# Seven-product groups of a fused attention + mixer block: 96-row operand tails, a plan table inside each group, ten tiles instead of eleven summed in DRAM

## The chip, the cores and the metric

The kernel runs on one core of a Trainium2 chip. The metric is the time of one execution in device microseconds (us); lower is better. A core has a matrix engine (TensorE, PE in the profile, with its weight loads shown as PEld), three engines for elementwise work (VectorE = DVE, ScalarE = ACT, GpSimd = POOL) and SyncE (SP), which in this kernel only issues DMA transfers. Every engine works through its own instructions in program order, and each instruction waits for the semaphores of what it depends on.

## The reference, cut to what matters

x is (1, 2048, 576), F = 4608, 32 heads of 18 columns.

```python
xn = layernorm(x)
# A: sliding, dilated attention: each token looks back 8 places, 2 apart
q, k, v = heads(layernorm-input xn @ wqkv)      # 32 heads, Dh = 18
o  = softmax(q . k[s - 0, s - 2, ..., s - 14] * Dh**-0.5) @ v
A  = o @ wo
# B: mixer MLP
h  = gelu(layernorm(xn) @ w1); hs = spatial_shift(h) @ w2     # shifts +1 -1 +2 -2
x1 = xn + hs
B  = x1 + gelu(layernorm(x1) @ w3) @ w4          # w3: 576 x 4608, w4: 4608 x 576
out = x + A + B
```

## The kernel before, in words

All matrix products are made from two fp32r parts: an operand is held as a high part (a cast) and a low part (the operand minus its high part), and high·high + high·low + low·high is summed in PSUM. So each operand costs a cast, which ACT makes, and a subtraction, which DVE makes, before PE may use it.

The time falls into stages: wqkv, w1 and w2 with the layer norms (to about 315 us); then 48 *units* (`for u, (c, b) in enumerate(units)`), which take the first half of F in twelve chunks `c` of 256 hidden columns by four blocks `b` of 512 tokens; then twelve *groups* (`for q in range(NQ)`), which take the second half of F; eight more products behind the groups (the tail); and the last phase, the attention output times wo (L212, sixteen token tiles).

**A unit** makes two `up` products (14 matmuls of 128x512 each, L795), whose gelu ACT takes out of PSUM twice, as the high part (L778) and in full (L779); DVE makes the low part (L789). It then makes four `down` products (12 matmuls of 128x288, L808) with the hidden columns of the unit before. The `down` results are summed per token tile, in one of two ways: for the tiles of `YD` (11 of 16) ACT copies PSUM to a staging buffer (L812) and POOL issues a DMA that accumulates it into DRAM (L813); for the other tiles DVE adds PSUM to a tile that stays in SBUF (L816). PSUM holds a few such results, so PE waits when an eviction is late.

The attention runs meanwhile on DVE, as the generator `attention`: `bg(r)` is called at the places between the products of a unit and lets DVE take so many microseconds of attention work each time (by fixed prices in the generator; RATE[0]/6 = 1.4 per call). What is left of it after the units is issued in one piece (`while not state["done"]: bg(1e9)`), behind the last unit and ahead of the groups. Its last step is a DMA `od<-o`.

**A group** `q` takes a chunk pair of F for one half of the tokens (q 0 to 5 the first half, 6 to 11 the second). Instead of eight block products it makes seven, P1 to P7 (`product`, L1011, 7 matmuls of 128x512 each), of sums of the w3 blocks with sums of the x blocks:

- the *w side*: `load_pair` loads a pair of raw w3 blocks (`w3st`), `split_a` splits the blocks that are used as they are (`w3a`: casts L899 to L901 on ACT, low parts L903 and L904 on DVE), `combine` makes the sums in place on DVE (L893), `split_s` splits these sums (`w3s`). `w3a` has two buffers, `w3s` one, so `split_s` of the next group can begin only when the last product of the present group is done;
- the *x side*: seven operands B11, B21, T1 to T4, B22, the same for all six groups of a half. `get_op` loads one (an SP DMA), `split_op` splits it (ACT L865, L866 and L873, DVE L587). They are loaded for q = 0 and, while the first half ends, for q = 6;
- the products' combinations are additions on DVE (`z_add`, L1015), then four gelus (L784, L785) with their low parts (L789), and eight `down` products D0 to D7 with the hidden columns of the group before.

Every block has 288 rows: two tiles of 128 and a *tail* of 32. HALVES packs the three tail terms into one matmul: the 32 tail rows are stacked as high, low, high against high, high, low in slots of 32 partitions; before, there are four slots (128 rows), the last two making up the doubled term.

The order in which PE takes these is in the lists ORDER, SWAP (q = 6) and FIRST (q = 0, four downs only). What the other engines do between them hangs on `if` lines behind each item: `split_a` at D2 and D3, `combine` at D3, `split_s` at D5 and D6, w4's split (L560, L562) at D5 and D6, w4's load at D0, the pair of two groups on at D2. In q = 7 to 10 the attention output of a block of 512 tokens is loaded tile by tile (`load_o`, `ot`, two buffers, SP), turned on DVE (`o_turn`: L158, L159) and written back (`put`, four DMAs `xd<-st`). In q = 11 and behind it these blocks are read back (`get`), split (`split_x`, L178 to L184) and wo is loaded and split (`load_wo`, `split_wo`, L197, L198), in the same two buffers `ot`. SP issues its DMAs in program order and has eight semaphores for them, so a ninth waits until an earlier one has landed.

## Time and profile before

| | |
|---|---|
| three runs | 1398.01, 1395.32, 1397.78 us; median 1397.78 us |
| profiled execution | 1397.48 us |
| its span, first to last instruction | 1395.7 us |
| mean granted TensorE clock | 0.968 |
| busy: PE, PEld | 1306.2 us (94%), 1190.6 us (85%) |
| busy: DVE, ACT, POOL | 956.2 us (69%), 585.0 us (42%), 228.4 us (16%) |
| mean DMA rate over the span | 157 GB/s |
| units u = 4 to 43 | 367.9 to 876.9 us |
| twelve groups and the tail | 930.06 to 1332.86 us |
| last phase (L212) | 1332.86 us to the end |

In the rows of the profile a name such as `cc<-xt,w3s` gives what an instruction writes and reads; L is the line in the listing above; x is a count; a bracket [7.69 <-DVE w3s L903] says that the engine stood idle for 7.69 us ahead of the instruction and what ended that. "1.75 ... x7" is a row of seven matmuls that took 1.75 us together.

### The profile page before, as it was taken

To read this page: it belongs to the slowest core of one execution; us is meant where nothing else is said; L and a number is where in the kernel's file an instruction comes from. 1 tells how busy PE (TensorE), PEld (TensorE's weight loads), DVE (VectorE), ACT (ScalarE), POOL (GpSimd) and SP (SyncE) were. 2 spreads that over 40 slices of the span, in tenths; PEclk is the share of its full clock that TensorE was granted. 3 is DMA by queue.
4 is the path that set the end of the run, shared out by engine and by line. 5 is a ranking of instruction groups with operands and counts; after the bars stand their busy time and mean duration, and the time that the engine had idled before them with its cause. 6 is when DMAs were issued, how large, how long until landed. Compare 5 with 4: busy or idle time off the path is not lost.

```text
span 1395.7 us, 19602 instructions
## 1 busy us (share of the span) xinstructions
PE 1306.2 (94%) x7594; PEld 1190.6 (85%) x7594; DVE 956.2 (69%) x1315; ACT 585.0 (42%) x937; POOL 228.4 (16%) x329
## 2 busy tenths in 40 slices
PE   8999999999999999999999999975999889777799
PEld 8999998997899999999999999964788768666698
DVE  6455626775558988898889878987656686555431
ACT  4232246345443434433434343563546584333610
POOL 2111100111212212222222211210112111111200
PEclk9999999999999999999999999996999999988899
DMA  8538764168778897968786947865556766677962
GB/s 215 149 102 169 168 158 122 54 193 217 177 198 158 160 230 141 197 130 197 127 176 134 213 68 153 165 139 135 118 109 108 196 155 134 160 165 151 305 150 83
DMA packets 199524, 219.12 MB, mean 157 GB/s; under 512 B 76280, under 2 KB 134008, under 8 KB 199304
## 3 DMA queue, kind: packets, MB, share of 16 engines
q1 hardware_dynamic: 166904, 151.51, 37.6%
q0 software_dynamic: 32528, 66.37, 31.2%
q8 instruction: 59, 0.97, 0.3%
q14 instruction: 33, 0.27, 0.1%
HBM read 116.29 MB, written 113.18 MB: 164 GB/s over the span
## 4 chain that ended last, share of the span: by engine, by line
PE 53%; issue 9%; DMA 5%; ACT 3%; DVE 3%; POOL 1%; SPq 1%; POOLq 0%; ACTq 0%; DVEq 0%
PE ps L808 24%; PE p L795 20%; PE cc L1011 5%; PE ps L212 4%; POOL yd L813 1%; DMA Y<-in_B_w_dram 1%; DMA x1n<-xn 1%; DMA ot<-in_A_wo_dram 1%; DMA w3st<-in_B_w_dram 1%; DVE o L707 1%; DVE xt L587 1%; DVE prod L703 1%; DMA yd<-Y 1%; ACT ev L812 0%; ACT c L784 0%
## 5 line engine op out<-in xcount | busy, mean ns | idle before, releaser
L808 PE MATMUL ps<-w,c 128*128 128x288 f32 x3456 | 488.1, 299 | 25.5 <-ACT Y L812 14.4
L808 PEld LDWEIGHTS ps<-w,c 128*128 128x128 f32 x3456 | 478.0, 192 | 38.4 <-ACT Y L812 16.6
L813 POOL DMA_DIRECT2D yd<-Y x141 | 124.4, 893 | 497.7 <-ACT Y L812 480.8
L812 ACT COPY Y<-ps 128x576 f32<-128x576 f32 x141 | 89.9, 640 | 152.6 <-PE ps L808 84.9
L789 DVE TENSOR_TENSOR c<-Y,c 128x512 fp32r<-128x512 f32 x144 | 98.7, 686 | 80.1 <-ACT Y L779 78.6
L778 ACT ACTIVATE c<-p 128x512 fp32r<-128x512 f32 x96 | 57.6, 600 | 189.2 <-PE p L795 189.2
L212 PE MATMUL ps<-WQ,xt 128*128 128x432 f32 x672 | 134.8, 360 | 0.0
L212 PEld LDWEIGHTS ps<-WQ,xt 128*128 128x128 f32 x672 | 125.6, 188 | 5.7
L1011 PE MATMUL cc<-xt,w3s 128*128 128x512 f32 x252 | 76.2, 451 | 50.5 <-DVE w3s L903 40.7
L1011 PEld LDWEIGHTS cc<-xt,w3s 128*128 128x128 f32 x252 | 54.0, 220 | 67.0 <-DVE w3s L903 42.5
L813 POOL DMA_DIRECT2D yd<-ev x57 | 49.7, 878 | 292.4 <-ACT ev L812 283.3
L723 DVE TENSOR_TENSOR prod<-q,k 128x1152 f32<-128x1152 f32 x64 | 86.6, 1353 | 0.8
L726 DVE TENSOR_REDUCE L<-prod 128x64 f32<-128x1152 f32 x64 | 86.4, 1350 | 0.8
L795 PE MATMUL p<-xt,w3a 128*128 128x512 f32 x336 | 80.3, 396 | 1.9 <-ACT Y L779 1.9
L795 PE MATMUL p<-x1n,w3a 128*128 128x512 f32 x336 | 79.7, 394 | 0.0
L795 PE MATMUL p<-x1n,w3s 128*128 128x512 f32 x336 | 78.6, 390 | 0.0
L795 PE MATMUL p<-xt,w3s 128*128 128x512 f32 x336 | 78.5, 390 | 0.0
L1015 DVE TENSOR_TENSOR Y<-cc,Y 128x512 f32<-128x512 f32 x84 | 55.6, 684 | 32.4 <-PE cc L1011 31.5
L795 PEld LDWEIGHTS p<-xt,w3a 128*128 128x128 f32 x336 | 63.5, 191 | 15.4 <-ACT Y L779 2.3
L707 DVE TENSOR_TENSOR o<-o,prod 128x1152 f32<-128x1152 f32 x56 | 75.8, 1354 | 1.0
L703 DVE TENSOR_TENSOR prod<-v,L 128x1152 f32<-128x1152 f32 x56 | 75.7, 1352 | 0.7
L795 PEld LDWEIGHTS p<-x1n,w3a 128*128 128x128 f32 x336 | 63.4, 191 | 13.0
(177 smaller groups left out, 1804.2 us busy)
## 6 DMA issues: line engine op xcount, KB each, us to landing
yd<-Y POOLq DMA_DIRECT2D x141, 288.0 KB, 5.1
yd<-ev POOLq DMA_DIRECT2D x57, 288.0 KB, 6.8
Y<-in_B_w_dram SPq DMA_DIRECT2D x24, 576.0 KB
w3st<-in_B_w_dram SPq DMA_DIRECT2D x46, 256.0 KB
qkvd<-stg SPq DMA_DIRECT2D x24, 432.0 KB
xd<-st SPq DMA_DIRECT2D x32, 320.0 KB
xin<-in_A_x_dram SPq DMA_DIRECT2D x16, 288.0 KB
xt<-xd SPq DMA_DIRECT2D x6, 768.0 KB
```

The costliest lines, as they stand in the source:

```text
L212: pe.matmul(ps[:, h, :n], xs(a), ws(b, h), start=i == 0, stop=i == len(PAIRS) - 1)
L703: dve.tensor_tensor(dst, vv, Lf[:, :, w:w + 1].to_broadcast([128, TPP * GH, HD]), op=ALU.mult)
L707: dve.tensor_tensor(o, o, dst, op=ALU.add)
L723: dve.tensor_tensor(prod.rearrange("p (j h) d -> p j (h d)", h=GH), q, k[:, r0:r0 + TPP, :], op=ALU.mult)
L726: dve.tensor_reduce(Lf[:, :, w], prod, axis=AX.X, op=ALU.add)
L778: act.activation(by_token(h[:, 0, :]), in_order(ps), AF.Gelu_apprx_tanh)
L789: dve.tensor_tensor(h[:, 1, :], g, h[:, 0, :].bitcast(F32), op=ALU.subtract)
L795: pe.matmul(ps, W3[f][:, w, :], x1n[b][:, a, :], start=n == 0, stop=n == len(PAIRS) - 1)
L808: pe.matmul(ps[:, k, :HF], h[:, col], w[:, p, k * HF:(k + 1) * HF], start=n == 0, stop=n == len(seq) - 1)
L812: act.copy(e.rearrange("p (h c) -> p h c", h=2), ps[:, :, :HF])
L813: pool.dma_start(yd[t], e, accum_op=ALU.add)
L1011: pe.matmul(ps, WX[w][:, v, SLOT[w], :], area[xk][:, a, :], start=i == 0, stop=i == len(HALVES) - 1)
```

## The change

- **Tails of 96 rows.** `get_op`, `load_pair` and `product` take three slots of 32 rows instead of four. `split_op` needs one ACT cast and one DVE subtraction less, `split_ws` one ACT cast less; `combine` does the body and the tail of each sum in separate instructions (8 instead of 4).
- **A plan.** For each group a dictionary `plan` says which casts, sums, gelus and loads stand behind which product. `split_a`'s casts move from D2 to P2, its low parts to P6; `combine` to D0; `split_s` starts at P3 and ends at D3 (before: D5 and D6); the second gelu goes from D4 to D5; w4's split ends at D7.
- **Four buffers** for the attention output's tiles, loaded three ahead (before: two), with a `put` at D7; wo's rows get their own buffers in a pool of their own, loaded from the start of q = 11.
- **YD** has ten tiles instead of eleven, others than before, with five staging buffers instead of seven; SCR is gone.
- **Smaller moves.** RATE[0] 8.8 instead of 8.4; `get_n(1)` one tile earlier; the first w3 and w4 loads at u = 1; `split_n(3)`'s first half one product later; q = 5 loads the next half's operands ahead of the group's other steps.

```diff
-YD = (1, 3, 5, 6, 7, 8, 9, 11, 13, 14, 15)
+YD = (1, 2, 3, 5, 7, 9, 10, 11, 13, 15)
...
-    RATE = [8.4, 2.0]
+    RATE = [8.8, 2.0]
...
-        sp.dma_start(dst[:, 0, :],
-                     dram_ap(src, 256 * 512, [[0, 4], [512, 32], [1, 512]]))
+        sp.dma_start(dst[0:96, 0, :], dram_ap(src, 256 * 512, [[0, 3], [512, 32], [1, 512]]))
...
-            pe.matmul(ps, WX[w][:, v, SLOT[w], :], area[xk][:, a, :], start=i == 0, stop=i == len(HALVES) - 1)
+            k = 128 if a else 96
+            pe.matmul(ps, WX[w][:k, v, SLOT[w], :], area[xk][:k, a, :], start=i == 0, stop=i == len(HALVES) - 1)
...
-            dve.tensor_tensor(st[:, :, o, :], st[:, :, o, :], st[:, :, i, :], op=op)
+            dve.tensor_tensor(st[:, 1:3, o, :], st[:, 1:3, o, :], st[:, 1:3, i, :], op=op)
+            dve.tensor_tensor(st[0:96, 0, o, :], st[0:96, 0, o, :], st[0:96, 0, i, :], op=op)
...
-        r = worw[k] = opool.tile([128, D], F32, name="ot", bufs=2)
+        r = worw[k] = wopool.tile([128, D], F32, name="wr", bufs=2)
...
-        otile[t] = opool.tile([128, D], F32, name="ot", bufs=2)
+        otile[t] = opool.tile([128, D], F32, name="ot", bufs=4)
...
     def o_turn(t):
+        if t + 3 < NT:
+            load_o(t + 3)
         turn(otile[t], t % 4)
...
+        elif z < -1:
+            plan = {"P2": [run(split_a, n, (0, 1))], "P6": [run(split_a, n, (2,))],
+                    "D0": [run(load_w4, p), run(combine, n)], "P3": [run(split_s, n, (0,) if q != NWP else (0, 1))],
+                    "D2": [run(split_s, n, (1,))] if q != NWP else [], "D3": [gelu22, run(split_s, n, (2,))],
+                    "D4": [low22], "D5": [gelu12], "D6": [low12, run(split_w4, p, 0)],
+                    "D7": [run(split_w4, p, 1)]}
...
+        if z == -1:
+            late("P2", lambda: read_xo(0, xp_tile(2)))
+            late("P5", lambda: read_xo(1, ring_block(("o", 1))))
+            late("P7", lambda: read_xo(2, xp_tile(3)))
+            late("P3", lambda: read_xo(3, ring_block(("o", 3))))
...
+            for f in plan.get(it, ()):
+                f()
```

How the instructions stand now, at three places.

**DVE between the last unit and the third product of q = 0.** `o` and `prod` are the attention's tiles (L703, L707); `w3s` is what P6 of q = 0 waits for. Before, the end of the piece that was left of the attention (nine more such rows stand ahead of these):

```order
L703 TENSOR_TENSOR prod<-v,L 128x1152
L707 TENSOR_TENSOR o<-o,prod 128x1152
L703 TENSOR_TENSOR prod<-v,L 128x1152
L707 TENSOR_TENSOR o<-o,prod 128x1152
L903 TENSOR_TENSOR w3s<-w3st,w3s 128x1024
L904 TENSOR_TENSOR w3s<-w3st,Y 64x512
L1015 TENSOR_TENSOR Y<-cc,Y 128x512
L816 TENSOR_TENSOR Y<-ps,Y 128x576
```

The same place now:

```order
L587 SCALAR_TENSOR_TENSOR xt<-xt 128x1024
L587 SCALAR_TENSOR_TENSOR xt<-xt,Y 32x512
L898 TENSOR_TENSOR w3s<-w3st,w3s 128x1024
L899 TENSOR_TENSOR w3s<-w3st,w3s 32x512
L1012 TENSOR_TENSOR Y<-cc,Y 128x512
L816 TENSOR_TENSOR Y<-ps,Y 128x576
L1012 TENSOR_TENSOR Y<-cc,Y 128x512
```

No attention instruction is left there; the last one now stands inside the unit u = 43.

**DVE in a group with attention tiles (q = 8).** L158/L159 are a turn of `ot`, `w3a` and `w3s` the low parts for the next group, `w3st` the sums (`combine`). Before:

```order
L158 STREAM_TRANSPOSE st<-ot 128x16x32
L159 STREAM_TRANSPOSE st<-ot 128x4x32
L903 TENSOR_TENSOR w3a<-w3st,w3a 128x768
L904 TENSOR_TENSOR w3a<-w3st,Y 64x384
L893 TENSOR_TENSOR w3st<-w3st 128x3x128 x4
L158 STREAM_TRANSPOSE st<-ot 128x16x32
L159 STREAM_TRANSPOSE st<-ot 128x4x32
L789 TENSOR_TENSOR c_10577<-Y,c_10577 128x512
L816 TENSOR_TENSOR Y<-ps,Y 128x576
L903 TENSOR_TENSOR w3s<-w3st,w3s 128x1024
```

Now, from the end of `combine` on:

```order
L888 TENSOR_TENSOR w3st<-w3st 128x2x128
L889 TENSOR_TENSOR w3st<-w3st 96x128
L158 STREAM_TRANSPOSE st<-ot 128x16x32
L159 STREAM_TRANSPOSE st<-ot 128x4x32
L1012 TENSOR_TENSOR Y<-cc,Y 128x512 x2
L816 TENSOR_TENSOR Y<-ps,Y 128x576
L158 STREAM_TRANSPOSE st<-ot 128x16x32
L159 STREAM_TRANSPOSE st<-ot 128x4x32
L898 TENSOR_TENSOR w3s<-w3st,w3s 128x1024
L899 TENSOR_TENSOR w3s<-w3st,w3s 32x512
```

`combine` stands ahead of the group's first turn instead of between its second and third, and the low parts of `w3s` behind the second turn instead of behind the third.

**ACT in the group q = 10.** `ev` is a staging copy, `c` and the `Y` behind it a gelu. Before:

```order
L899 CAST w3a<-w3st 128x768
L900 CAST Y<-w3st 64x384
L901 CAST w3a<-w3st 64x384
L812 COPY ev<-ps 128x576
L784 ACTIVATE c_11072<-Y 128x512
L785 ACTIVATE Y<-Y 128x512
L812 COPY ev<-ps 128x576
L784 ACTIVATE c_11099<-Y 128x512
L785 ACTIVATE Y<-Y 128x512
L812 COPY ev<-ps 128x576
L899 CAST w3s<-w3st 128x1024
```

Now, the group's casts of `w3a` and what follows them:

```order
L894 CAST w3a<-w3st 128x768
L896 CAST w3a<-w3st 96x384
L784 ACTIVATE c_10947<-Y 128x512
L785 ACTIVATE Y<-Y 128x512
L812 COPY ev<-ps 128x576
L894 CAST w3s<-w3st 128x1024
L896 CAST w3s<-w3st 96x512
L812 COPY ev<-ps 128x576
L784 ACTIVATE c_11059<-Y 128x512
L785 ACTIVATE Y<-Y 128x512
```

The casts of `w3a` now stand ahead of the group's first gelu (between P2 and P5), and those of `w3s` ahead of the two last gelus instead of behind them and the downs.

More of the change, by code (lines that the diff above doesn't have):

```diff
@@ L945, in fused_block @@
                 get_n(3, x1n[3])
[L946 removed]
+            if (u, i) in ((1, 0), (2, 1)):
                 split_n(u + 1, x1n[u + 1], 0, RT)
@@ L969, in fused_block @@
         if c < NPL - 1:
-            if k == 0:
+            if u == 1 or k == 0 and u:
                 load_w3p(c + 1)
@@ L1075, in fused_block @@
         if z == -5:
-            load_o(0)
-            load_o(1)
+            for t in range(3):
+                load_o(t)
         if z == -1:
             evc_pool.__exit__(None, None, None)
-            EV[0] = (9, 11, 14, 8)
+            opc.__exit__(None, None, None)
+            EV[0] = (9, 11, 10)
             wop = tc.tile_pool(name="wop", bufs=1, reuse_waits="tile")
-            Wo = wop.__enter__().tile([128, 10, D], F32R, name="Wo")
+            wopool = wop.__enter__()
+            Wo = wopool.tile([128, 10, D], F32R, name="Wo")
             load_w4(p)
+            load_wo(0)
+            load_wo(1)
         if q == 0:
@@ L1096, in fused_block, with gelu22, gelu12 @@
             WX[o] = WS[q]
+        def gelu22():
+            hid[q, "c22"] = gelu_z("c22", Z1)
+        def gelu12():
+            hid[q, "c12"] = gelu_z("c12", Z2)
+        low22 = lambda: low_part(hid[q, "c22"], Z1)
+        low12 = lambda: low_part(hid[q, "c12"], Z2)
+        run = lambda f, *a: lambda: f(*a)
+        n = q + 1
+        if q == 0:
+            plan = {"D0": [run(load_w4, p)], "P5": [run(split_op, "T4")],
+                    "D1": [run(split_op, "B22")], "D2": [run(split_a, n)],
+                    "P4": [run(combine, n)],
+                    "D3": [gelu22, gelu12, run(split_s, n), low22, low12, run(split_w4, p),
+                           run(load_pair, 2)]}
+        elif z < -1:
[4 more added lines that the diff above has]
+                    "D7": [run(split_w4, p, 1)]}
+            if z < -2:
+                plan["D2"].append(run(load_pair, q + 2))
+        else:
+            plan = {"D1": [run(split_w4, p)], "D3": [gelu22], "D4": [gelu12, low22],
+                    "D5": [low12]}
+            for it, b, h in (("D2", 0, 0), ("D3", 0, 1), ("D5", 1, 0), ("D6", 1, 1)):
+                plan.setdefault(it, []).append(lambda b=b, h=h: split_x(xo[b], h))
+            for it, k in (("D4", 0), ("D7", 1)):
+                plan.setdefault(it, []).extend([run(split_wo, k), run(load_wo, k + 2)])
@@ new lines, in fused_block @@
+        late = lambda it, *fs: plan.setdefault(it, []).extend(fs)
+        if q == NWP - 1:
+            for it, k in zip(("P1", "P2", "P6", "P5", "P7", "P4", "P3"), OPS):
+                plan.setdefault(it, []).insert(0, run(get_op, 1, k))
+            for it, k in zip(("D0", "D2", "D4", "D6"), OPS):
+                late(it, run(split_op, k))
+        if q == NWP:
+            for it, k in zip(("P1", "P6", "P7"), OPS[4:]):
+                late(it, run(split_op, k))
+        if -5 <= z <= -2:
+            for i in range(4):
+                t = 4 * (z + 5) + i
+                late(f"D{2 * i}", run(o_turn, t))
+            late("D7", run(put, ("o", z + 5)))
```

161 lines of the change are left out of this document (34 added, 127 removed).

## The prediction

> **What bounds the kernel now.** I read the page first. It gives PE 94% of the span, so the time is PE's work and PE's gaps. Then the waits of PE, each row with what was waited for, the total in us, the count and the longest:
>
> ```profile
> span 1395.7 us, 19602 instructions
> ...
> PE cc L1011 <- DVE w3s L903: 40.7, 5, 17.8
> PE ps L808 <- ACT Y L812: 14.4, 8, 3.7
> PE ps L808 <- ACT ev L812: 7.1, 5, 2.9
> ```
>
> The largest, 40.7 us, is for one thing, the low parts of the sums of w3 (`w3s`), in five places. Where they lie shows PE's timeline (start, duration, what, and in brackets the idle time ahead of it):
>
> ```profile
> 930.06 3.36 PE L1011 MATMUL cc<-x1n,w3a 128*128 128x512 f32 x14
> ...
> 953.03 5.27 PE L1011 MATMUL cc<-xt,w3s 128*128 128x512 f32 x13 [17.79 <-DVE w3s L903]
> ...
> 974.05 3.55 PE L1011 MATMUL cc<-x1n,w3a 128*128 128x512 f32 x14
> ...
> 1004.01 3.37 PE L1011 MATMUL cc<-x1n,w3a 128*128 128x512 f32 x14
> ...
> 1080.08 3.37 PE L1011 MATMUL cc<-x1n,w3a 128*128 128x512 f32 x14
> ...
> 1119.32 0.73 PE L1011 MATMUL cc<-xt,w3s 128*128 128x512 f32 x2 [2.50 <-ACT xt L865]
> ...
> 1146.11 3.36 PE L1011 MATMUL cc<-x1n,w3a 128*128 128x512 f32 x14
> ...
> 1170.42 3.36 PE L1011 MATMUL cc<-x1n,w3a 128*128 128x512 f32 x14
> ...
> 1182.66 3.36 PE L1011 MATMUL cc<-xt,w3a 128*128 128x512 f32 x7 [2.54 <-DVE Y L1015]
> ...
> 1210.38 4.62 PE L1011 MATMUL cc<-xt,w3s 128*128 128x512 f32 x13 [7.69 <-DVE w3s L903]
> ...
> 1268.69 3.36 PE L1011 MATMUL cc<-x1n,w3a 128*128 128x512 f32 x14
> ...
> 1280.46 5.37 PE L1011 MATMUL cc<-xt,w3s 128*128 128x512 f32 x13 [8.18 <-DVE w3s L903]
> ...
> 1332.86 14.96 PE L212 MATMUL ps<-Wo,x1n 128*128 128x288 f32 x112
> ```
>
> The rows of 14 matmuls without a bracket start the groups q = 0, 1, 2, 5, 7, 8 and 11. From one to the next: q = 0 takes 44.0 us, q = 1 30.0, q = 2 to 4 together 76.1 (25.36 each), q = 5 and 6 66.0, q = 7 24.3, q = 8 to 10 98.3, and q = 11 with the tail 64.2. q = 7 has no gap, so 24.3 us is what a group's matmuls need, and what the others take beyond that is waiting and its consequence. The consequence is the clock: after the 17.79 us gap thirteen matmuls took 5.27 us, 405 ns each, where fourteen take 3.36 us, 240 ns each, in the running stream. A gap costs its own length and then up to 2.2 us more.
>
> **The change part by part.**
>
> *q = 0.* DVE's timeline says why w3s came late:
>
> ```profile
> 933.77 1.36 DVE L707 TENSOR_TENSOR o<-o,prod 128x1152 f32<-128x1152 f32 x1
> ...
> 951.76 1.22 DVE L903 TENSOR_TENSOR w3s<-w3st,w3s 128x1024 fp32r<-128x1024 f32 x1
> ```
>
> Thirteen instructions of the attention, 933.77 to 951.76, stand in front of w3s. In the changed order none is left there (first place shown above; RATE is 8.8 for 8.4), and the last stands in the unit u = 43. So 18.0 us of DVE work leave this place and PE's gap of 17.79 with its 2.2 us of slow matmuls goes. SP held the loads of T4, B22 and the next pair behind the attention's last `od<-o`, which goes as well. What is left: the matmuls of seven products and four downs instead of eight. A down takes 12 of the 24 matmuls of the row below, 1.7 us, so 24.3 − 4 × 1.7 = 17.5 us, and I add 1.5 us for the operands T4 and B22, which are split while DVE still has w3s to do. 44.0 to 19: **−25**.
>
> *q = 1 to 4.* Each of these groups shows one such wait:
>
> ```profile
> 1000.74 3.44 PE L808 MATMUL ps<-w,c 128*128 128x288 f32 x24 [1.04 <-ACT ev L812]
> ```
>
> It is the eviction behind the casts of `w3s`, which move from D5 to P3, ahead of it. 25.36 − 24.31 = 1.05 us a group; I take three of them (q = 2 to 4), **−3**, and leave q = 1 as it is, since in q = 0 all casts still stand together at D3.
>
> *q = 5 and 6.* 66.0 us against 48.6 without waits. These load and split the second half's operands; the row at 1119.32 shows PE waiting for ACT's split of one of them. The change issues the loads earlier, but ACT keeps nearly all its work, and `w3a`'s casts now stand ahead of those of T4 and B22 in q = 6. Bounds: −6, if a third of the 17 us goes; +5, if ACT waits for the next pair's landing at P2. I take **+2**.
>
> *q = 8 to 10.* Around the longest wait but one, SP and DVE:
>
> ```profile
> 1193.30 10.62 SPq L886 DMA_DIRECT2D w3st<-in_B_w_dram  x1
> ...
> 1207.05 0.71 DVE L158 STREAM_TRANSPOSE st<-ot 128x512 f32<-128x512 f32 x1 [6.68 <-DMA ot<-od]
> ...
> 1209.12 1.21 DVE L903 TENSOR_TENSOR w3s<-w3st,w3s 128x1024 fp32r<-128x1024 f32 x1
> ```
>
> SP stood 10.62 us in one issue, the tiles of the attention output behind it came late, and DVE, in order, held the low part of w3s (at D6) behind a turn (at D4) that waited 6.68 us for its tile. Two edits hit this: tiles are loaded three turns ahead instead of two, and w3s's low parts stand behind the second turn, at D3. The turn in front of them then uses a tile asked for some 10 us sooner. The three groups go from 98.3 to 3 × 24.3, plus 2 us that I leave for pairs landing behind the writes of `put`: 75. **−23**.
>
> *q = 11 and the tail.* Matmuls: 24.3 + 8 × 1.7 = 37.9 of 64.2 us. The 8.18 us gap at its start is the same as in q = 8 to 10 and goes, with the slow matmuls after it. The rest is the tail, where
>
> ```profile
> 1307.14 12.75 DMA ot<-in_A_wo_dram
> ...
> 1319.92 0.67 ACT L197 CAST Wo<-ot 128x576 fp32r<-128x576 f32 x1 [7.57 <-DMA ot<-in_A_wo_dram]
> ...
> 1321.18 2.09 PE L808 MATMUL ps<-w,c 128*128 128x288 f32 x12 [3.48 <-ACT Y L812]
> ```
>
> ACT waits 7.57 us for a row block of wo that was 12.75 us on its way, and the eviction behind it holds PE 3.48 us. wo now has buffers of its own and starts with q = 11; but the reads of the attention output (four blocks of 5 x 128 x 512 fp32, 1.31 MB each) begin earlier too, and the third block of wo waits behind them on SP. The window
>
> ```profile
> 1268.70:1332.90 64.20, 46.63 (x244) 41.97 (x243) 34.24 (x46) 33.09 (x49) 11.32 (x13) 0.81 0.88 228
> ```
>
> has the DMA engines 88% busy at 228 GB/s (the last two columns). 5.2 MB of reads at that rate are 23 us. Between 37.9, if all is hidden, and 60, if only the gap goes, I take 48: **−16**.
>
> *Units, and the smaller items.* First the forty units u = 4 to 43 (the columns after the length are PE, PEld, DVE, ACT and POOL busy), then two groups of DVE's instructions in that window, then two of those behind it, to 952 us:
>
> ```profile
> 367.90:876.90 509.00, 509.00 (x3042) 463.85 (x3041) 428.47 (x426) 202.93 (x323) 113.12 (x129) 1.00 0.78 160
> ```
>
> ```profile
> L789 DVE TENSOR_TENSOR c<-Y,c 128x512 fp32r<-128x512 f32 x80 | 55.2, 689 | 65.8 <-ACT Y L779 65.7
> L816 DVE TENSOR_TENSOR Y<-ps,Y 128x576 f32<-128x576 f32 x49 | 36.7, 749 | 0.0
> ```
>
> ```profile
> L707 DVE TENSOR_TENSOR o<-o,prod 128x1152 f32<-128x1152 f32 x14 | 19.0, 1356 | 0.3
> L703 DVE TENSOR_TENSOR prod<-v,L 128x1152 f32<-128x1152 f32 x14 | 19.0, 1355 | 0.3
> ...
> L893 DVE TENSOR_TENSOR w3st<-w3st 128x384 f32<-128x384 f32 x4 | 2.2, 557 | 0.1
> ```
>
> L707 and L703 are DVE's attention work behind 876.9 us, 38.0 us; it comes into the window of the forty units. So do some 11 sums (160 downs, 60 of them on DVE instead of 49) at 0.749, 8.2 us. DVE's work there goes from 428.5 to 474.7 of 509.0 us. It is hidden if DVE's waits shrink from 80.5 to 34.3 us. Of the waiting, 65.7 us are waits for a gelu just issued, which vanish by themselves when DVE runs later. But the load is uneven: of 40 windows of one unit's length DVE was busy for under 7 us in four, like the first row below, and up to 12.7 in others, like the second.
>
> ```profile
> 800.50:813.30 12.80, 5.99 (x9) 1.00 0.48 77
> ...
> 749.60:762.40 12.80, 12.66 (x13) 1.00 0.33 47
> ```
>
> The 46.2 us come on top of the full units above all, 1.2 each, so that DVE has next to nothing spare between the slack ones and PE will wait now and then. I take a tenth of the bound: all waits staying, 474.7 + 80.5 = 555.2 would be +46, none 0, so **+4**.
>
> The 96-row products I cost at 0 as well: the count of matmuls and of columns stays the same, and no row here shows a matmul of fewer rows. `combine` in eight instructions costs DVE little: four of 557 ns now (2.2 us); eight of them, each smaller, can't cost more than 4.5, and in q = 7 DVE was busy for 17.7 of 24.3 us (row below, columns as above), so the 2.3 are covered; without that cover, in eleven groups, they would be 25 us. One cast less per split frees ACT a little, off the path.
>
> ```profile
> 1146.10:1170.40 24.30, 24.30 (x147) 21.95 (x146) 17.70 (x29) 12.27 (x22) 4.36 (x5) 1.00 0.61 125
> ```
>
> *Sum.* −25 − 3 + 2 − 23 − 16 + 4 = −61. The profiled execution took 1397.5 us (1.8 beyond its span) and the median of the runs is 1397.8, the same within 0.3. 1397.5 − 61 = **1336.5 us**.
>
> *One rule against a row.* At 1182.66 seven matmuls took 3.36 us, 480 ns each, right after a wait of only 2.54 us: such a gap costs about 4.2 us in all. The Trainium skill, "TensorE: Matmul & The Clock Gate", section "HAM oscillation — how this bites in real kernels", has the clock fall for idle gaps over about 3.4 us. By that rule short gaps keep their bare length, and the waits of 2 to 3 us left in q = 5 and 6 would weigh some 3 us less than I leave them; the row disagrees with it, and the sum goes by the row.
>
> **The rivals.**
>
> *DVE becomes the bound of the units.* For it: 93% of the window busy, and one-sided waits (PE needs the low parts and the sums of the same engine). Against it: the waits are mostly for gelus that are early enough for an engine that runs late. If half of the bound comes true, +23 instead of +4: 1355 us.
>
> *The tail stays DMA-bound.* For it: 88% busy there, and 23 us of reads ahead of wo. Then only the 8.18 us gap and some of its slow matmuls go, −5 instead of −16: 1348 us.
>
> *q = 8 to 10 keep their waits.* If the tiles come late whatever their place, because SP stands in the pairs' loads as at 1193.30, the gap moves from w3s's low part to the next turn and is paid there; I give half of the 23 back: 1348 us.
>
> *The other side: ACT waits at P2.* In ten groups (q = 1 to 10) ACT now casts `w3a` right after the copy of P1 instead of at D2, from a pair that is loaded one group earlier. If it has not landed, every gelu and eviction behind it waits. ACT's and SP's timelines in q = 2:
>
> ```profile
> 1007.72 0.42 SPq L884 DMA_DIRECT2D w3st<-in_B_w_dram  x1
> ...
> 1008.46 0.63 ACT L784 ACTIVATE c<-Y 128x512 fp32r<-128x512 f32 x1 [1.94 <-DVE Y L1015]
> ...
> 1016.96 0.64 ACT L812 COPY ev<-ps 128x576 f32<-128x576 f32 x1 [7.20 <-PE ps L808]
> ...
> 1020.69 0.83 ACT L899 CAST w3a<-w3st 128x768 fp32r<-128x768 f32 x1
> ```
>
> ACT idles 1.94 + 7.20 us around there, and the casts (0.83 for the body, the tail less) take under 1.7 of it, so about 7.5 us of late landing are free; beyond, each us is PE's. To come out slower than before, ten groups must lose the 61 us, 6.1 each: the pair must land 13.6 us after P2. From the issue at 1007.72 to the next group's P2, about 1032 (its start is 25.36 us behind 1004.01), are 24 us, so a landing must take 38. With 10 us lost in each group the time is 1436 us. Against it: at 12.75 us, as the row of wo above, a pair lands 11 us ahead of P2. The Trainium skill, "TensorE: Matmul & The Clock Gate", section "Architectural detail: the array is 16× 32×32, not 1× 128×128", calls the queues of ACT and DVE strict FIFO, which is the mechanism; the rows at 1319.92 and 1207.05 agree, with 7.57 and 6.68 us in which nothing behind passed.
>
> **How the numbers follow.** My forecast (within 10 us) 0.53; better, with the waits of q = 5 and 6 half gone and the tail nearly hidden, 1319 us, 0.09; DVE the bound of the units 0.16; the tail 0.10; q = 8 to 10 0.06; ACT at P2 0.06, of which 0.02 end near no change. The range, 1316 to 1362 us, holds all but the last and the worse half of DVE's. A change below 0.2% (2.8 us) can't be told from none here. Faster: 0.94; the same: 0.02; slower: 0.04.
>
> **What would show it.** Right: q = 0 near 19 us with no wait over 2 us for w3s; q = 8 to 10 near 25 each; units at most 5 us longer with DVE 93% busy; q = 11 and tail under 50. Wrong: gaps in the units for L789 or L816; ACT idle at P2 with a DMA as releaser; PE waiting for an eviction behind wo's casts in the tail.

## The result, and the profile after

The changed kernel took 1343.08 us (median of four runs, 1338.77 to 1350.14) against 1396.58 us before (1395.32 to 1398.01): a ratio of 0.9622, 95% interval 0.9574 to 0.9669, so 53.5 us less. The profiled execution took 1340.4 us (span 1338.6), 57 us less than the one of before. The runs of the changed kernel lie further apart than those of before, 0.8% against 0.2%.

PE's waits, as at the head of the prediction:

```profile
span 1338.6 us, 19508 instructions
...
PE cc L1008 <- ACT xt L864: 12.1, 2, 7.5
PE ps L808 <- ACT Y L812: 10.7, 5, 4.3
PE ps L808 <- DVE Y L816: 7.0, 3, 3.6
PE ps L808 <- ACT ev L812: 4.4, 6, 0.7
PE p L795 <- DVE w3s L198: 3.8, 1, 3.8
...
PE cc L1008 <- DVE w3s L898: 0.8, 1, 0.8
```

The 40.7 us for w3s are down to 0.8 (the last row; L898 is the old L903). The largest wait is now for ACT's split of an x operand (L864 is the old L865), in one group alone. PE's timeline, the rows that start a group and the long waits:

```profile
931.86 1.79 PE L1008 MATMUL cc<-x1n,w3a 128*128 128x512 f32 x7
...
950.11 3.39 PE L1008 MATMUL cc<-x1n,w3a 128*128 128x512 f32 x14
...
977.43 3.40 PE L1008 MATMUL cc<-x1n,w3a 128*128 128x512 f32 x14
...
1049.49 3.40 PE L1008 MATMUL cc<-x1n,w3a 128*128 128x512 f32 x14
...
1074.95 3.39 PE L1008 MATMUL cc<-x1n,w3a 128*128 128x512 f32 x14
...
1087.40 3.76 PE L1008 MATMUL cc<-xt,w3s 128*128 128x512 f32 x7 [7.45 <-ACT xt L864]
...
1100.76 3.76 PE L1008 MATMUL cc<-xt,w3a 128*128 128x512 f32 x7 [4.61 <-ACT xt L864]
...
1118.52 3.40 PE L1008 MATMUL cc<-x1n,w3a 128*128 128x512 f32 x14
...
1142.54 3.40 PE L1008 MATMUL cc<-x1n,w3a 128*128 128x512 f32 x14
...
1192.55 2.18 PE L808 MATMUL ps<-w,c 128*128 128x288 f32 x12 [3.58 <-DVE Y L816]
...
1227.09 3.40 PE L1008 MATMUL cc<-x1n,w3a 128*128 128x512 f32 x14
...
1265.53 3.25 PE L808 MATMUL ps<-w,c 128*128 128x288 f32 x12 [4.14 <-ACT Y L812]
...
1275.95 14.97 PE L212 MATMUL ps<-Wo,x1n 128*128 128x288 f32 x112
```

From one start to the next, in us (the last stage ends with the span):

| | before | after | difference | predicted |
|---|---|---|---|---|
| up to q = 0 | 930.1 | 931.9 | +1.8 | +4 |
| q = 0 | 44.0 | 18.3 | −25.7 | −25 |
| q = 1 | 30.0 | 27.3 | −2.6 | 0 |
| q = 2 to 4 | 76.1 | 72.1 | −4.0 | −3 |
| q = 5 | 31.8 | 25.5 | −6.3 | |
| q = 6 | 34.2 | 43.6 | +9.3 | +2 with q = 5 |
| q = 7 | 24.3 | 24.0 | −0.3 | 0 |
| q = 8 to 10 | 98.3 | 84.6 | −13.7 | −23 |
| q = 11 and tail | 64.2 | 48.9 | −15.3 | −16 |
| last phase | 62.8 | 62.7 | −0.2 | 0 |
| sum | 1395.7 | 1338.6 | −57.1 | −61 |

Two places fell out otherwise than the prediction had them. In q = 6, ACT:

```profile
1085.24 1.15 ACT L560 CAST w<-Y 128x1152 fp32r<-128x1152 f32 x1 [10.80 <-DMA Y<-in_B_w_dram]
1086.30 1.05 ACT L864 ACTIVATE xt<-xt 128x1024 fp32r<-128x1024 f32 x1
...
1097.75 0.83 ACT L894 CAST w3a<-w3st 128x768 fp32r<-128x768 f32 x1 [4.63 <-DMA w3st<-in_B_w_dram]
```

ACT stands 10.80 us for w4, with the split of an operand right behind it, and PE's 7.45 us end with that split; then it stands 4.63 us at P2 for the pair, and PE's 4.61 us follow. And around q = 9, SP and then DVE:

```profile
1167.98 15.39 SPq L166 DMA_DIRECT2D xd<-st  x4
```

```profile
1189.75 0.71 DVE L158 STREAM_TRANSPOSE st<-ot 128x512 f32<-128x512 f32 x1 [7.50 <-DMA xd<-st]
...
1191.75 0.74 DVE L816 TENSOR_TENSOR Y<-ps,Y 128x576 f32<-128x576 f32 x1
```

The four DMAs of `put` took SP 15.39 us to issue. The group's first turn overwrites the buffer `st` that they read, and waits 7.50 us; the sum that PE waits for stands behind it on DVE. What DVE waits for from q = 7 to the end of the tail, before and after:

```profile
DVE st L158 <- DMA ot<-od: 40.9, 9, 7.0
DVE st L158 <- DMA xd<-st: 11.9, 3, 4.4
```

```profile
DVE st L158 <- DMA xd<-st: 10.5, 3, 7.5
```

The tiles (`ot`) are no longer waited for at all; the put's buffer is, as long as before.

### The profile page after: what moved, and what is told of

Its sections match the earlier page's. It is cut to its first block, busy times and chain, and to the rows that moved or that the text cites. A ratio compares the mean times of both kernels' runs of the same rounds, so it can differ in the third digit from the quotient of the medians.

```text
span 1338.6 us, 19508 instructions
## 1 busy us (share of the span) xinstructions
PE 1288.4 (96%) x7594; PEld 1180.0 (88%) x7594; DVE 957.5 (72%) x1368; ACT 552.0 (41%) x881; POOL 211.8 (16%) x310
## 4 chain that ended last, share of the span: by engine, by line
PE 56%; issue 8%; DVE 5%; DMA 2%; POOL 1%; ACT 1%; SPq 1%; POOLq 0%; DVEq 0%; ACTq 0%
PE ps L808 26%; PE p L795 20%; PE cc L1008 6%; PE ps L212 4%; POOL yd L813 1%; DVE prod L703 1%; DMA w3st<-in_B_w_dram 1%; DVE o L707 1%; DMA v<-qkvd 1%; DMA yd<-Y 1%; DVE c L789 0%; SPq L879 0%; DVE Y L816 0%; DVE Y L1012 0%; DVE w3st L888 0%
## 5 line engine op out<-in xcount | busy, mean ns | idle before, releaser
L808 PE MATMUL ps<-w,c 128*128 128x288 f32 x3456 | 482.2, 297 | 22.1 <-ACT Y L812 10.7
L813 POOL DMA_DIRECT2D yd<-Y x128 | 112.9, 885 | 490.0 <-ACT Y L812 468.4
L789 DVE TENSOR_TENSOR c<-Y,c 128x512 fp32r<-128x512 f32 x144 | 98.9, 687 | 75.1 <-ACT Y L779 57.1
L812 ACT COPY Y<-ps 128x576 f32<-128x576 f32 x128 | 81.8, 640 | 165.9 <-PE ps L808 97.8
L816 DVE TENSOR_TENSOR Y<-ps,Y 128x576 f32<-128x576 f32 x108 | 81.1, 752 | 6.7 <-PE ps L808 6.3
L813 POOL DMA_DIRECT2D yd<-ev x52 | 45.3, 872 | 248.7 <-ACT ev L812 247.5
L795 PE MATMUL p<-x1n,w3s 128*128 128x512 f32 x336 | 80.4, 396 | 3.8 <-DVE w3s L198 3.8
L795 PEld LDWEIGHTS p<-x1n,w3s 128*128 128x128 f32 x336 | 63.5, 191 | 17.2 <-DVE w3s L198 4.2
L1008 PE MATMUL cc<-xt,w3s 128*128 128x512 f32 (+1 forms) x252 | 64.8, 402 | 12.7 <-ACT xt L864 7.5
L707 DVE TENSOR_TENSOR o<-o,prod 128x1152 f32<-128x1152 f32 x56 | 75.8, 1354 | 0.9
L703 DVE TENSOR_TENSOR prod<-v,L 128x1152 f32<-128x1152 f32 x56 | 75.7, 1352 | 0.4
L1012 DVE TENSOR_TENSOR Y<-cc,Y 128x512 f32<-128x512 f32 x84 | 56.0, 686 | 27.9 <-PE cc L1008 27.3
```

Of the source, the lines that this page charges most:

```text
L703: dve.tensor_tensor(dst, vv, Lf[:, :, w:w + 1].to_broadcast([128, TPP * GH, HD]), op=ALU.mult)
L707: dve.tensor_tensor(o, o, dst, op=ALU.add)
L789: dve.tensor_tensor(h[:, 1, :], g, h[:, 0, :].bitcast(F32), op=ALU.subtract)
L795: pe.matmul(ps, W3[f][:, w, :], x1n[b][:, a, :], start=n == 0, stop=n == len(PAIRS) - 1)
L808: pe.matmul(ps[:, k, :HF], h[:, col], w[:, p, k * HF:(k + 1) * HF], start=n == 0, stop=n == len(seq) - 1)
L812: act.copy(e.rearrange("p (h c) -> p h c", h=2), ps[:, :, :HF])
```

## The experiments

Theory: the time comes from the attention's leftover (q = 0), from the tile buffers (q = 8 to 11) and from the plan's places; what was not gained lies in transfers that hold ACT or DVE, which work in order. The rivals stand with each run. Group lengths are read as above. Each ratio is to the kernel before, run beside it on the same chip; the changed kernel's is 0.9622. Its interval, 0.9574 to 0.9669, takes in every run's ratio but those of 1, 2 and 6: by the whole time only these three differ from it. The others are read stage by stage, each from one profiled execution. How alike such readings are shows in the kernels whose edit leaves a stage alone: the unit u = 4 begins at 362.4 to 367.9 us, q = 1 takes 27.3 to 30.0, q = 2 to 4 always 72.06, q = 6 43.6 to 45.6, q = 8 to 10 84.2 to 89.7, q = 11 with the tail 48.5 to 52.5. These ranges are called the spread below.

**1. RATE[0] back at 8.4, in the changed kernel.**

```diff
-    RATE = [8.8, 2.0]
+    RATE = [8.4, 2.0]
```

> The changed kernel with RATE[0] back at 8.4: the attention's end stands again between the last unit and w3s's low part in q = 0. Theory (that piece of DVE work alone makes q = 0's 25 us): q = 0 goes from 18.3 back to 38 to 44 us with a wait of about 17 us for w3s, and the 3.8 us wait for w3s L198 at 882 us goes with its slow matmuls, about -5: in all 1355 to 1367 us. Rival (the gain of q = 0 is that of the new places of its splits and loads): q = 0 stays under 25 us, 1337 to 1348 us.

1364.25 us, ratio 0.9781 (0.9756 to 0.9807). The groups begin at 925.6 instead of 931.9, and q = 0 takes 40.0 us:

```profile
947.04 3.35 PE L1008 MATMUL cc<-xt,w3s 128*128 128x512 f32 x7 [16.26 <-DVE w3s L898]
```

So the new places of q = 0's steps are worth at most 4 us (40.0 against 44.0) while the attention stands there; the theory holds. The units cost 6.3 us for getting 21.8 back in q = 0; counted from the start of u = 4 on, they cost 5.8.

**2. The same one number, in the kernel before.**

```diff
-    RATE = [8.4, 2.0]
+    RATE = [8.8, 2.0]
```

> The kernel before with one edit, RATE[0] 8.8: no attention instruction is left behind the units. Theory: q = 0 falls from 44 to about 20 us, the units grow by 0 to 3 us since DVE has eleven sums less there than in the changed kernel, the groups after stay: 1371 to 1377 us. Rival (DVE is the bound of the units): the units grow by 10 us or more, 1382 us and above.

1374.38 us, ratio 0.9840 (0.9823 to 0.9856). q = 0 takes 18.4 us, the groups begin at 934.0 instead of 930.1. One number in one line is thus worth 21 us of the 54. Of these 4.0 us 1.0 lies ahead of u = 4, which begins at 369.03 instead of 368.02. The units grow by 3.0, the theory's bound and far from the rival's 10.

**3. q = 5: w4 and the pair are loaded ahead of the x operands.**

```diff
+            plan["D0"].pop(0)
+            plan["D2"].pop()
+            plan["P1"][:0] = [run(load_w4, p), run(load_pair, q + 2)]
```

> The changed kernel; in q = 5 alone the loads of w4 and of the next w3 pair are issued at P1, ahead of the seven x operands instead of among and behind them. Theory (q = 6 waits because ACT, in order, stands for w4's and the pair's landing ahead of the casts of T3 and T4): the waits of 7.45 and 4.61 us go, q = 5 and 6 fall from 69 to 52 to 57 us, the time by 12 to 17 us. Rival (the DMA engines are simply full in q = 5): the x operands land 5 to 8 us later, their splits hold ACT instead, q = 5 and 6 stay within 5 us of 69.

1339.45 us, ratio 0.9602 (0.9579 to 0.9625). q = 6 falls from 43.6 to 34.6 us, but q = 5 grows from 25.5 to 32.0: 66.6 together instead of 69.0. ACT's row in q = 5:

```profile
1067.79 1.06 ACT L864 ACTIVATE x1n<-x1n 128x1024 fp32r<-128x1024 f32 x1 [10.23 <-DMA x1n<-xn]
```

Now the first x operand comes late and holds ACT for 10.23 us. What is issued first arrives first, and the rest waits: the rival's result, within its 5 us. Its cause, full DMA engines, fits q = 5 of the changed kernel alone. The last two columns of these rows, for q = 5 and q = 6, are the DMA engines' busy share and GB/s:

```profile
1049.50:1074.95 25.45, 24.28 (x147) 21.95 (x146) 21.61 (x33) 17.79 (x28) 4.24 (x6) 1.00 0.90 212
1074.95:1118.50 43.55, 28.99 (x147) 24.08 (x146) 23.51 (x35) 21.50 (x32) 4.45 (x6) 0.84 0.56 142
```

In q = 6 they are busy 56% of the time, so what holds it is single transfers that come late, and not full engines throughout.

**4. The turns of a group at D4 to D7.**

```diff
-                late(f"D{2 * i}", run(o_turn, t))
+                late(f"D{4 + i}", run(o_turn, t))
```

> The changed kernel; the four turns of a group stand at D4, D5, D6, D7 instead of D0, D2, D4, D6. Theory (the first turn of a group waits for the writes of the last put, which still read the buffer st, and holds DVE): q = 8 to 10 fall from 84.6 to 73 to 77 us, the time by 8 to 12 us. Rival (tiles that land late, or DVE's load late in a group, make the waits): the wait moves to the later turns and holds the gelus' low parts and w4's split, q = 8 to 10 stay above 81 us.

1344.17 us, ratio 0.9628 (0.9614 to 0.9643). q = 8 takes 24.0 us instead of 26.0, q = 9 30.7 instead of 32.5, q = 10 28.2 instead of 26.0, and the tail gets 4.6 us longer, 1.0 beyond the spread. The 83.0 us of the three groups are above the rival's 81 and only 1.2 below the spread. DVE now waits 9.55 us for the last tile of q = 8, since each load moved with its turn. Inconclusive for the put; run 9 repairs that.

**5. The plan taken back, all else kept.**

```diff
-            plan = {"P2": [run(split_a, n, (0, 1))], "P6": [run(split_a, n, (2,))],
...
+            plan = {"D0": [run(load_w4, p)], "D2": [run(split_a, n, (0, 1))],
+                    "D3": [gelu22, run(split_a, n, (2,)), run(combine, n)], "D4": [gelu12],
+                    "D5": [run(split_s, n, (0, 1)), run(split_w4, p, 0), low22],
+                    "D6": [run(split_s, n, (2,)), low12, run(split_w4, p, 1)]}
```

> The changed kernel with the steps of a group (w3a's casts, the sums, w3s's split, the gelus, w4's split) back where they stood before, in q = 1 to 10; the four tile buffers, the ten tiles of YD, the 96-row tails and RATE stay. Theory (the plan takes the eviction wait of 1.05 us out of each of q = 1 to 4 and the w3s waits out of q = 8 to 11; in q = 6 it costs the 4.6 us in which the casts of w3a wait for their pair): q = 2 to 4 go back to 25.3 us each, w3s waits of 2 to 6 us return in q = 9 to 11, q = 6 gains 3 to 6 us: 1342 to 1358 us. Rival (all of the gain in q = 8 to 11 is the tile buffers'): q = 8 to 11 stay, the time ends below 1343 us.

1343.25 us, ratio 0.9611 (0.9595 to 0.9627): the same time as with the plan. q = 2 to 4 take 24.76 us each instead of 24.02 (theory: 25.3), q = 5 26.7, but q = 6 only 35.9 instead of 43.6. No wait for w3s returns in q = 9 to 11, which the theory had expected: with four tile buffers the plan is not needed for its absence. q = 8 to 11 are 6 us longer in this execution, with other waits (4.58 us for a sum of DVE in q = 10); but in run 3, whose edit ends with q = 5, they are 5 us longer too, so this does not speak against the rival. The plan as a whole earns nothing here: q = 2 to 5 and 7 gain 4.5 us by it and q = 6 loses 7.7.

**6. Two tile buffers, two loads ahead.**

```diff
-        if t + 3 < NT:
-            load_o(t + 3)
         turn(otile[t], t % 4)
+        if t + 2 < NT:
+            load_o(t + 2)
```

> The changed kernel with two buffers for the tiles of the attention output and each load issued behind a turn, two ahead, as before; the plan stays. Theory (three ahead with four buffers took 40.9 us of DVE's waits for tiles away): DVE waits again for tiles, 15 us or more in q = 7 to 10, and these groups lengthen by 6 to 14 us in all: 1349 to 1357 us. Rival (the plan's places for w3s's low part alone make the gain): q = 8 to 10 stay within 3 us of 84.6.

1357.44 us, ratio 0.9707 (0.9693 to 0.9722). q = 8 to 10 take 96.9 us instead of 84.6, and DVE waits as before:

```profile
DVE st L158 <- DMA ot<-od: 40.9, 8, 11.9
```

The theory holds: the buffers are worth 12 us in these groups, 7 against the longest of the spread. The tail's 52.8 us instead of 48.9 are no finding by the spread. No wait for w3s returns here either. PE now waits for w4's split on DVE, which stands behind the turns:

```profile
PE ps L808 <- DVE w L562: 12.3, 3, 5.2
```

That is how the prediction's rival for q = 8 to 10 had it: with late tiles and the new places the gap moves on and is paid elsewhere.

**7. The put in rows of 10 KB.**

```diff
-            sp.dma_start(dram_ap(xd[key], 128 * q, [[512, 32], [32 * 512, 20], [1, 128]]),
-                         ST[32 * q:32 * q + 32])
+            sp.dma_start(dram_ap(xd[key], 32 * q * 2560, [[2560, 32], [1, 2560]]),
+                         ST[32 * q:32 * q + 32].rearrange("p j c -> p (j c)"))
```

> The changed kernel; the attention's blocks are written back in rows of 10 KB per partition instead of pieces of 512 bytes, the same bytes, into the same buffer (so the blocks read back later are in the wrong order, and the attention's part of the output is not the reference's). Theory (the first turn of a group waits for the put's landing, and the put is slow by its 2560 pieces): SP's 15 us on the four issues fall to under 5, DVE's waits for xd<-st go, q = 8 to 10 fall from 84.6 to 74 to 79 us: 1332 to 1338 us. Rival (the DMA engines are full by bytes there): the put takes as long and the groups stay within 3 us.

1338.10 us, ratio 0.9582 (0.9565 to 0.9598). The put that had held SP for 15.39 us:

```profile
1166.73 5.72 SPq L167 DMA_DIRECT2D xd<-st  x4
```

q = 9 takes 26.0 us instead of 32.5. But the next put still takes 9.06 us, a turn in q = 10 waits 5.90 for it, and q = 8 to 10 come to 82.9 us, 1.3 below the spread; 79 us at most was expected and not reached. SP's time fell with the longer rows, but what the groups gain by it is not clear of the spread. Nor is the size of the pieces all that holds SP. The same four DMAs in pieces of 512 bytes took this in the kernel before, and this in run 6:

```profile
1181.46 4.34 SPq L166 DMA_DIRECT2D xd<-st  x4
```

```profile
1187.96 6.08 SPq L166 DMA_DIRECT2D xd<-st  x4
```

In the kernel before the three puts issued in q = 8 to 10 take SP 4.3 us each; in the changed kernel the first three take 9.75, 15.39 and 14.08. So the put became slow with the change, and the prediction had no term for that. What makes it slow, such as the tile loads that are now issued just ahead of it, no run separates.

**8. The eleven tiles of YD of before.**

```diff
-YD = (1, 2, 3, 5, 7, 9, 10, 11, 13, 15)
+YD = (1, 3, 5, 6, 7, 8, 9, 11, 13, 14, 15)
```

> The changed kernel with the eleven tiles of YD of before (staging and scratch tiles moved accordingly). Theory (of the 3.8 us wait at 882 us two thirds come from the eleven sums that DVE took over in the units; ACT, POOL and the DMA queues have room for the evictions): the wait falls to about 1 us, the units by 3 to 5 us, the groups stay within 3 us: 1335 to 1342 us. Rival (eighteen accumulations fewer relieve the DMA engines in q = 5 to 11): these groups lengthen by 5 us or more, and the time is not below 1343 us.

1350.11 us, ratio 0.9659 (0.9644 to 0.9673). The wait at 882 us is under 1 us and the groups begin 1.3 us earlier (3.1 less from the start of u = 4 on); q = 8 to 10 even fall to 80.4 us. But q = 11 with the tail grows from 48.9 to 59.5 us, with these waits of PE:

```profile
PE ps L808 <- ACT Y L812: 11.5, 6, 4.5
PE cc L1008 <- DVE Y L1012: 2.4, 1, 2.4
PE cc L1008 <- DVE w3s L898: 2.0, 1, 2.0
```

The 59.5 us are 7 beyond the spread. In this stage 14.98 MB move instead of 12.96; at its 250 GB/s, with the DMA engines 94% busy, the difference is an estimated 8 us. The theory had the units right and the rest wrong. By its numbers the rival holds (q = 5 to the tail take 7.8 us more), but the value of one tile less lies in the tail, which neither had named alone. Since the staging tiles move with YD, the run can't split that between fewer accumulations and other staging.

**9. Turns at D4 to D7, each load four tiles ahead.**

```diff
-        if t + 3 < NT:
-            load_o(t + 3)
         turn(otile[t], t % 4)
+        if t + 4 < NT:
+            load_o(t + 4)
...
-                late(f"D{2 * i}", run(o_turn, t))
+                late(f"D{4 + i}", run(o_turn, t))
```

> The changed kernel; the turns of q = 7 to 10 stand at D4, D5, D6, D7 as in turnslate, but each is followed by the load of the tile four turns on, so that a tile has a whole group to land. Theory (a group's first turn waits for the last put, and in turnslate the tile needed at D7 was asked for only at D4): the waits for xd<-st and for ot<-od both go, q = 8 to 10 take 73 to 77 us instead of 84.6, 1331 to 1337 us. Rival (the DMA engines of q = 8 to 10 are full, whatever the order): DVE waits for one or the other for 8 us or more in all, q = 8 to 10 stay above 80 us.

1348.54 us, ratio 0.9649 (0.9624 to 0.9674). DVE waits 14.0 us for xd<-st, q = 8 to 10 take 86.3 us: the rival's result. Its cause is not shown, for the DMA engines are 75% busy over these groups, at 175 GB/s. In q = 9 and 10 ACT now waits for w4, 4.55 us and then 11.26:

```profile
1207.45 1.15 ACT L560 CAST w<-Y 128x1152 fp32r<-128x1152 f32 x1 [11.26 <-DMA Y<-in_B_w_dram]
```

w4 is issued behind the put on SP and comes late. Wherever the turn stands, some transfer of the group ends too late for the engine that meets it in order. So the order of the turns alone does not remove the loss.

**10. 128-row tails in the loads and the products.**

```diff
-            k = 128 if a else 96
+            k = 128
```

> The changed kernel with 128-row tails in the loads and the products: the loads bring four slots again, the matmuls of the tails take 128 rows, the fourth slot of the w side is set to zero by POOL (so the result is the same sum). The saved casts and subtractions stay. Theory (96 rows save PE nothing; a quarter less of the tails' bytes is under 2% of what the DMA engines move there): groups without waits keep 24.0 us, all groups together within 4 us, 1339 to 1348 us. Rival (rows or bytes count): a group without waits takes 24.3 us or more, or q = 5 and 6 lengthen by 5 us, 1348 us or above.

1345.65 us, ratio 0.9633 (0.9617 to 0.9649). A group without waits takes 23.88 us, against 24.02 with 96 rows. The matmuls of the changed kernel in q = 2 to 4, by shape, where the mean is the number behind the busy time:

```profile
L1008 PE MATMUL cc<-xt,w3s 128*128 128x512 f32 x54 | 13.9, 393 | 0.0
...
L1008 PE MATMUL cc<-xt,w3s 96*128 96x512 f32 x9 | 3.6, 395 | 0.0
```

96 rows take 395 ns, 128 rows 393. No gain on PE and, in a group, 0.14 us lost. q = 6 and the tail are 2.7 us longer each with 128 rows, q = 6 0.7 beyond the spread and the tail within it; whether the smaller loads help there stays open.

**11. q = 6 alone with its old places.**

```diff
+            if q == NWP:
+                plan = {"D0": [run(load_w4, p)], "D2": [run(split_a, n, (0, 1))],
...
```

> The changed kernel; in q = 6 alone the steps stand where they stood before (casts of w3a at D2, sums at D3, w3s's split at D5 and D6). Theory (in q = 6 ACT, in order, stands at P2 for a pair that has not landed, and holds the split of T4): the wait of 4.61 us before P4's product goes, that of 7.45 us, which comes from w4's load, stays; q = 6 takes 35 to 39 us instead of 43.6, 1335 to 1340 us. Rival (ACT's amount of work in q = 6 sets it): the wait moves to P3 or the downs, q = 6 stays above 41 us.

1338.19 us, ratio 0.9579 (0.9565 to 0.9594). q = 6 takes 37.1 us instead of 43.6. The product that had waited 4.61 us has no wait, the one of 7.45 us keeps it:

```profile
1087.64 3.76 PE L1008 MATMUL cc<-xt,w3s 128*128 128x512 f32 x7 [7.91 <-ACT xt L864]
...
1096.60 1.79 PE L1008 MATMUL cc<-xt,w3a 128*128 128x512 f32 x7
```

The theory holds in both halves: at P2 ACT held the split of T4 for the pair's sake. (The edit moves all of the plan's steps in q = 6, so the 6.4 us are not P2's alone.) It is the fastest of the kernels that compute all of the reference, though its interval overlaps that of the changed kernel.

**12. Three edits in three stages.**

```diff
-    RATE = [8.8, 2.0]
+    RATE = [8.7, 2.0]
...
-        r = worw[k] = wopool.tile([128, D], F32, name="wr", bufs=2)
+        r = worw[k] = wopool.tile([128, D], F32, name="wr", bufs=5)
...
+            late("P3", run(load_wo, 2), run(load_wo, 3), run(load_wo, 4))
```

and q = 6 as in run 11.

> Three edits of the changed kernel in three stages that don't overlap: q6old's order in q = 6; RATE[0] 8.7 for 8.8, with which the attention's last instruction stands two units later and still inside them; five buffers for wo's rows, whose last three loads are issued right behind the last read of the attention output instead of at D7 and in the tail. Theory: q = 6 takes 36 to 38 us as in q6old; the wait for w3s L198 at 882 us falls under 1.5 us and the units by 3 to 5 us; ACT no longer waits for wo, PE's wait of 4.1 us in the tail goes and q = 11 with the tail takes 43 to 46 us instead of 48.9: 1328 to 1333 us in all, faster than the kernel before and than the changed one. Rival (the tail is bound by the bytes of its reads, the units by DVE's work): wo lands as late as before and the tail keeps its wait, the units stay: 1336 to 1340 us.

1338.66 us, ratio 0.9599 (0.9584 to 0.9614), the same as run 11 alone. In the units the theory holds for the wait, 0.75 us instead of 3.77, and the groups begin 2.5 us earlier (2.6 less from the start of u = 4 on); q = 1 is 4 us longer, 3.25 of it waiting for casts of w3s. In the tail the rival holds. The third block of wo, ACT's row after and in this run:

```profile
1262.89 0.67 ACT L197 CAST Wo<-wr 128x576 fp32r<-128x576 f32 x1 [3.83 <-DMA wr<-in_A_wo_dram]
```

```profile
1260.96 0.67 ACT L197 CAST Wo<-wr 128x576 fp32r<-128x576 f32 x1 [5.42 <-DMA wr<-in_A_wo_dram]
```

It was issued at 1245.4 instead of 1252.9 and used at 1260.96 instead of 1262.89, in a stage that had begun 3.7 us earlier: nothing gained. An earlier issue does not bring wo earlier. With the DMA engines 92% busy over this stage, at 249 GB/s, it is likely that the tail waits for bytes; no run takes bytes alone away.

## Why the prediction was right, and where not

**q = 0 (−25, measured −25.7): right, and shown.** Runs 1 and 2 move 21 us with one number each, in both kernels.

**The sum (−61, measured −57.1): closer than its parts.** The three groups q = 8 to 10 and q = 5 and 6 came out 10 us worse than forecast, and the stages up to q = 0, q = 1 and q = 2 to 4 6 us better, of which q = 1's 2.6 are within the spread. That these offset each other is luck. Two of the prediction's signs of being wrong did appear, each in one place: ACT idle at P2 behind a DMA (4.63 us, q = 6), and PE waiting for an eviction behind a cast of wo in the tail (4.14 us; the eviction itself stood last for its staging buffer, 1.27 us).

**Units (+4, measured +1.8): right in kind, and not where I put it.** DVE's work and its waits in the forty units are now these (the window ends 1.6 us behind them):

```profile
366.00:876.90 510.90, 510.90 (x3050) 465.35 (x3049) 465.44 (x464) 199.78 (x315) 104.75 (x120) 1.00 0.75 158
```

```profile
DVE c L789 <- ACT Y L779: 29.5, 32, 2.7
DVE o L703 <- DMA v<-qkvd: 9.0, 1, 9.0
```

465.4 us of DVE were done (474.7 expected), and the waits for a gelu shrank from 65.7 to 29.5 as argued. The price is one wait, not many, and it comes behind the forty units, in u = 44:

```profile
875.30 3.60 PE L795 MATMUL p<-x1n,w3s 128*128 128x512 f32 x15
882.67 4.84 PE L795 MATMUL p<-x1n,w3s 128*128 128x512 f32 x13 [3.77 <-DVE w3s L198]
```

The low part of w3 (w3s L198) starts at 881.80 on DVE, right behind an attention instruction that starts at 880.53. The forty units take 509.2 us (366.11 to 875.30), against 509.1 before. From there to q = 0 it is 3.6 us more than before, close to the forecast +4. The 1.9 us that came back lie ahead of u = 4, whose start alone spreads over 5.5 us.

**q = 1 (0) and q = 2 to 4 (−3, measured −4.0): right; the cause only in part.** q = 1's −2.6 are within the spread. In q = 2 to 4 the plan is worth 0.74 us a group (run 5), not the 1.05 that I gave the casts; the rest of the 1.34 was not traced to an edit. The 24.3 us that I took from q = 7 as what a group's matmuls need were 0.3 too many: its last 72 matmuls took 10.12 us and take 9.69 now, with no wait listed in either.

**q = 5 and 6 (+2, measured +3.0): the sum right, its working wrong.** I had bounds of −6 and +5 for the two together. In fact q = 5 gained 6.3 and q = 6 lost 9.3. Of the loss 6.4 us belong to the rival *ACT waits at P2* (run 11), which I had weighed in all ten groups: it came true in one, the one whose pair was issued behind fourteen loads of operands. What is left there is the wait behind w4's late landing (7.91 us in run 11), which run 3 could only exchange for another. The rival's condition was right. Its place was not: I should have asked for the longest queue ahead of a pair, not for the usual one. The Trainium skill, "TensorE: Matmul & The Clock Gate", section "Architectural detail: the array is 16× 32×32, not 1× 128×128", has ACT's queue as strict FIFO; the rows at 1085.24 and 1097.75 agree, with 10.80 and 4.63 us of standing and, behind each, an operand's split that had no wait of its own.

**q = 8 to 10 (−23, measured −13.7): the step that failed.** "3 × 24.3, plus 2 us that I leave for pairs landing behind the writes of `put`" priced the put by what it delays behind it on SP. Its own buffer was forgotten: the first turn of a group waits for it, 7.50 us in q = 9, and PE then 3.58. The wait is in the trace of before, 11.9 us under `xd<-st`; I had read only the 40.9 us next to it. That the put would take SP 15.39 us where it had taken 4.34 had no term either. That the tile buffers take those 40.9 us away is shown (run 6: 12 us in the groups). Of the 12.5 us that the three groups take beyond 3 × 24.02, 8.5 lie in q = 9. The other 4 lie in q = 8 and q = 10, whose only waits of PE are two of 0.73 us each for an eviction (ACT ev L812, among the waits at the head of the result). The forecast had none of these; they are gone, and q = 8 takes 24.0 us, with the turns later (runs 4 and 9) or YD's old tiles (run 8). The remainder in q = 9 is no single wait: gone for the put it comes back for a tile (run 4), or for the put and w4 (run 9). How much of it is bytes and how much SP's order was not separated.

**q = 11 and tail (−16, measured −15.3): right, by a sum of two parts that I did not price apart.** Other kernels with the same steps there take up to 52.5 us, so the gain is 12 to 16 us and the profiled execution stands near its better end. Taking YD's old tiles back alone costs 10.7 us here (run 8), 7 of it beyond the spread, so a good part of the 16 is the lighter accumulation and its staging, which I had costed only as sums for DVE. That wo waits behind 5.2 MB of reads, as I said, fits run 12. One sum of the forecast does not close: 64.2 less the 8.18 us gap is 56.0, so my bound of 60 and the rival's −5, with only the gap gone, should have been 56 and −8.

**96 rows (0): right** for PE (run 10). The Trainium skill, "TensorE: Matmul & The Clock Gate", section "🎯 Why this matters for your kernels", says that a single matmul with K = 32 takes the time of K = 128; 395 against 393 ns agree with it for K = 96.

**Short gaps and the clock.** I let a gap of 2 to 3 us cost 4.2, by the row at 1182.66. In q = 6 now:

```profile
1109.32 1.43 PE L1008 MATMUL cc<-xt,w3s 128*128 128x512 f32 x5 [2.43 <-DVE xt L587]
```

Five matmuls at 286 ns, a granted clock of 1.00 over that stretch, against 480 ns and 0.51 after the 2.54 us gap of before. So a gap of this length may cost its bare length or much more; the rule that I set the row against fits this one and not that.

## What to carry to other kernels

A leftover of background work, drained in one piece between two stages, costs its whole length when the next stage's first step runs on the same engine; look for it before any finer placing. An operation moved earlier in an in-order engine's program is safe only if its data lands in time in the *worst* of the stages it is moved in. And where a stage's waits all end with transfers, taking one away can hand it to whoever meets the next late transfer, so price such a stage by all its transfers, in the order in which they are issued, and not by its present longest wait.

## What was not expected of the hardware

How long SP stands in the same four DMAs differs widely. The put of 1.31 MB in pieces of 512 bytes took 4.34 us in the kernel before, 6.08 in run 6 and 15.39 in the changed kernel, with the DMA engines 68 to 74% busy in all three; in rows of 10 KB, at nearly the same place of the changed program, it took 5.72. So longer rows shorten it where it is long, and short pieces alone do not make it long. The Trainium skill, "DMA: Bandwidth & Descriptors", section "Specifications", gives 512 bytes as the least piece for full rate; no run here measures that rate, only how long SP stood.

In a stretch with a clock of 1.00 a matmul of 96 rows among matmuls of 128 made a group of seven products 0.14 us longer (24.02 us in the changed kernel, 23.88 in run 10), 0.02 us for each.
